# Weight decoding after attention: scaling and casts from GpSimd to ScalarE, a landing count for decode steps, two x pieces made early

## The chip, the cores and the metric

The kernel runs on one core of a Trainium2 chip. TensorE (PE) multiplies matrices; VectorE (DVE), ScalarE (ACT) and GpSimd (POOL) work elementwise; SyncE (SP) issues most DMAs. Each engine takes its instructions in program order, and an instruction that waits holds up all that stand behind it on its engine. The metric is the device time of one execution in microseconds (us).

## The reference

It computes three stages in float32 on 2304 tokens (4 batches of 576) of width 512.

```python
# attention with random features, 8 heads of 64, 128 features
q_p, k_p = phi(q * scale), phi(k * scale)   # phi: exp(proj - sq - max) / sqrt(m)
num = q_p @ (k_p^T v); den = q_p @ sum(k_p)
x = num / (den + 1e-6)
# block 1: 512 -> 2048 -> 512
h = x @ w_in
y = (max(h, 0) + alpha * min(h, 0)) @ w_out
# block 2: 512 -> 1536 -> 512
out = ((y @ w_a) * (y @ w_b)) @ w_out2
```

The weights reach the chip as 64-bit values, in which float64 bit patterns stand (`in_w`, two 32-bit words to each), and are turned to float32 on the chip.

## The kernel before

**Precision.** TensorE multiplies in a format of fewer bits, so each operand is split into a high piece (a cast) and a low piece (the rest), and each product takes three matmuls: high by high, high by low, low by high. `xh`/`xl`, `gh`/`gl` are such pairs; a weight's pair lies in a slot tile `w`.

**Stages.** First, attention steps run beside block 1's first 1280 tokens in chunks of 256 (object `A`, to about 256 us of the profile). Then block 1 goes on in chunks of 256 or 512 tokens (object `X`): tokens 1280 to 2303 with hidden blocks 0 to 7, then all tokens with blocks 8 to 15, to about 548 us. For each hidden block there are 12 matmuls into `h`, then ScalarE `u` and `h`, VectorE `h`, ScalarE `gh`, VectorE `gl`, and 12 matmuls into `y`, one or two blocks later. At the end of a chunk `y` is copied (`yo`) or added (`yp`). Last comes block 2, in three weight phases by three token groups of 768, nine groups in all: two times a `dual` (seven units of 12 matmuls, 384 wide, into the PSUM banks W, E and B, by a scheme of seven products instead of eight), then `back` (72 matmuls, 512 wide, into `o`). Sums `u`, `s`, `e` of those banks are copied by ScalarE and combined by VectorE.

**Decoder.** 68 weight pieces of 128x512 are decoded: SyncE loads `raw` (three buffers), GpSimd scales the high word into `z` (`start`), VectorE forms `a` and `c` by four instructions (`bits`), and then, for the first 32 pieces (`piece`), ScalarE casts the high piece and GpSimd or VectorE takes the difference and adds (`a<-a,w` and `w<-a,c`). For block 2 (`single`, and `quad` with sums of two pieces) a high piece is a GpSimd cast and the low piece a VectorE difference (`stage`); the pair goes straight into its slot where that is open, and else into a buffer `t` (three buffers), from there to DRAM (`store`, issued by `flush`), and later back into a slot (`fetch`).

**Order.** Every engine's order is that of the Python code. Decoding is a generator that is advanced between other work: after attention by `pace`, as long as VectorE's counted work is less than 1 us behind that of TensorE (`clock`, summed from fixed costs while the program is written). `pick` gives a difference to VectorE or GpSimd by the load counted for each. `upto` runs the generator until a piece that is needed is made.

Of the kernel before, what the change touches and what calls it, by code (L numbers as in the profile page):

```python
# [18 lines left out]
P = 128  # L19
# [15 lines left out]
CI = 256  # L35
# [24 lines left out]
FIRST = 32  # L60
SIDE = 0
# [3 lines left out]
def tile_kernel(ctx: ExitStack, tc: tile.TileContext, qT, kT, v1, omT, wbits, alpha, out):  # L65
# [106 lines left out]
    clock = {"pe": 0.0, "dve": 0.0}  # L172
# [26 lines left out]

    def behind():  # L200
        return clock["dve"] - clock["pe"]
# [3 lines left out]
    class Decoder:  # L205


        def __init__(self):
            self.free = {}
            self.raw = {}  # L210
            self.ready = 0
            self.made = set()
            self.next = 0
            self.credit = 0.0
            self.free_run = False
            self.gen = None
            self.z = {}
            self.ahead = True
            self.got = PB
            self.due = None  # L220
            self.direct = set()

        def load(self, i, after=False):
            if i < NP and i not in self.raw:
                raw = dec.tile([P, DM, 2], U32, tag="raw", name=f"raw{i}", bufs=3)
                if after:
                    after_dve(raw[:, :, 0].bitcast(F32))
                nc.sync.dma_start(out=raw.rearrange("p n t -> p (n t)"), in_=wbits[order[i]].bitcast(U32))
# [12 lines left out]

        def bits(self, i):
            self.start(i)
# [10 lines left out]
            if not fine and self.ahead and i + 1 < NP:  # L254
                self.start(i + 1)
# [18 lines left out]

        def stage(self, q, src, cut=None):

            if cut != 1 and self.open(q):
                self.direct.add(q)
            t = slots[place(q)][2] if q in self.direct else dec.tile([P, 2, 512], F32R, tag="t", name=f"t{q}_{cut}", bufs=3)
            if cut is not None:  # L280
                o = 256 * cut if q in self.direct else 0
                t = t[:, :, o:o + 256]
            self.flush()
            nc.gpsimd.tensor_copy(out=t[:, 0], in_=src)
            load["pool"] += 1.5
            yield
            yield
            vec(t[:, 1], src, t[:, 0].bitcast(F32), ALU.subtract)
            self.due = (q, cut, t)
            yield  # L290

        def flush(self):
            if self.due:
                q, cut, t = self.due
                if q not in self.direct:
                    dst = store[q] if cut is None else store[q][:, :, 256 * cut:256 * cut + 256]
                    nc.sync.dma_start(out=dst, in_=t.bitcast(F32))
# [8 lines left out]
        def single(self, i, q):  # L306
# [3 lines left out]
            self.start(i + 1)  # L310
            if self.kind(i + 1) == "quad":
                self.start(i + 2)
# [4 lines left out]
        def quad(self, i, q0, q1, q2, q3, m):  # L317
# [18 lines left out]
            self.start(i + 2)  # L336
            if self.kind(i + 2) == "quad":
                self.start(i + 3)
# [7 lines left out]
        def fetch(self):  # L346

            while self.got < PB + PH2 * QS:
# [3 lines left out]
                if q not in self.direct:  # L352
                    nc.sync.dma_start(out=slots[place(q)][2].bitcast(F32), in_=store[q])
# [69 lines left out]
        def upto(self, q):  # L423
            while q not in self.made:
                if not self.advance():
                    assert q in self.made, (q, self.next)
            if q >= PB:
                self.fetch()
                assert self.got > q, (q, self.got)
# [11 lines left out]
    class Mlp:  # L441
        def __init__(self, st, cap, ybufs, side=None):
# [4 lines left out]
            if not self.pair:  # L447
                self.px = pool(name=f"px{cap}", bufs=6)
            self.pg = pool(name=f"pg{cap}", bufs=3)
# [5 lines left out]
            self.xs, self.ys, self.gs, self.part = {}, {}, {}, {}  # L455
            self.half = {}
            self.q = []
            self.beside = None
            self.after = []
# [149 lines left out]
        def run(self, work, between, ready=lambda end, k: None):  # L609
# [8 lines left out]
            for ci, (ph, o, n, fs, lc) in enumerate(work):  # L618
# [8 lines left out]
                for i, f in enumerate(fs):  # L627
# [5 lines left out]
                    if i == 3 and ph == 1:  # L633
                        self.load_y(o, n)
            while self.q:
# [5 lines left out]
    st_a = ExitStack()  # L641
# [9 lines left out]
    pskv = rpool(st_a, name="pskv", bufs=1, space=PSUM)  # L651
# [230 lines left out]
    st_m = ExitStack()  # L882
    A = Mlp(st_m, CI, 2)
    st_z = ExitStack()
    psp[0] = rpool(st_a, name="ps", bufs=5, space=PSUM)
# [25 lines left out]
    with st_m:  # L911
# [35 lines left out]


# [16 lines left out]
        A.run(work0, beside, ready)  # L965
        while nxt_s[0] < steps:
            attn_more()
    st_a.close()
# [17 lines left out]
    def load_x(tp, k):  # L986
        stg = t_(xpools[0], f"st{k}", f"st{tp}_{k}", cols=4 * TN).rearrange("p (k n) -> p k n", k=2)
        nc.sync.dma_start(out=stg, in_=ypart[:, k::2, tp * 2 * TN:(tp + 1) * 2 * TN])
# [47 lines left out]
    st_w = ExitStack()  # L1036
    w2 = st_w.enter_context(tc.tile_pool(name="w2", bufs=1, side=RIGHT, reuse_waits="tile"))
    slots.update({i: pair_of(w2, i) for i in range(NS1, NS)})

    with ExitStack() as st:  # L1040
        X = Mlp(st, CB, 4, RIGHT)
# [15 lines left out]
    st_w.close()  # L1057
# [231 lines left out]
```

## Time and profile before

| what | value |
|---|---|
| median of 3 runs | 973.85 us (973.31 to 975.03) |
| the profiled execution | 974.33 us |
| its span | 972.6 us |
| PE busy in the span | 942.2 us, 97% |
| DVE, ACT, POOL busy | 71%, 48%, 29% |

The span reaches from the first to the last profiled instruction; 1.7 us of the execution's time lie around it. Matmuls overlap in the records, and one that runs slowly still counts as busy, so the busy share of PE alone does not tell how much time PE lost; the length of a stretch against its count of matmuls does.

### The profile page before, as it was taken

To read this page: it belongs to the slowest core of one execution; us is meant where nothing else is said; L and a number is where in the kernel's file an instruction comes from. 1 tells how busy PE (TensorE), PEld (TensorE's weight loads), DVE (VectorE), ACT (ScalarE), POOL (GpSimd) and SP (SyncE) were. 2 spreads that over 40 slices of the span, in tenths; PEclk is the share of its full clock that TensorE was granted. 3 is DMA by queue.
4 is the path that set the end of the run, shared out by engine and by line. 5 is a ranking of instruction groups with operands and counts; after the bars stand their busy time and mean duration, and the time that the engine had idled before them with its cause. 6 is when DMAs were issued, how large, how long until landed. Compare 5 with 4: busy or idle time off the path is not lost.

```text
span 972.6 us, 16848 instructions
## 1 busy us (share of the span) xinstructions
PE 942.2 (97%) x6486; PEld 844.3 (87%) x6486; DVE 691.9 (71%) x1348; ACT 462.4 (48%) x1130; POOL 282.8 (29%) x240
## 2 busy tenths in 40 slices
PE   7889999999999999999999999999999999999997
PEld 6778899989887878889888898999988899989895
DVE  5998855554498896678776978988675988274641
ACT  5877766654444534234334435443343443454532
POOL 3686710000088762122221201212234042110202
PEclk9999999999999999999999999999999999999999
DMA  7554322000133242315526665259837389623404
GB/s 297 167 161 148 132 75 78 23 24 24 44 95 122 87 149 65 112 38 169 203 103 251 223 227 205 88 206 393 317 108 218 111 216 351 191 38 93 56 11 65
DMA packets 49280, 138.15 MB, mean 142 GB/s; under 512 B 4528, under 2 KB 10928, under 8 KB 49200
## 3 DMA queue, kind: packets, MB, share of 16 engines
q1 hardware_dynamic: 43872, 127.51, 37.3%
q0 software_dynamic: 5184, 9.44, 6.5%
q8 instruction: 51, 0.84, 0.3%
q14 instruction: 29, 0.24, 0.1%
q10 hardware_dynamic: 144, 0.13, 0.0%
HBM read 89.87 MB, written 47.19 MB: 141 GB/s over the span
## 4 chain that ended last, share of the span: by engine, by line
PE 64%; DVE 12%; issue 8%; DMA 6%; ACT 4%; POOL 4%; SPq 0%; POOLq 0%; ACTq 0%; DVEq 0%
PE y L187 16%; PE h L187 15%; PE o L187 11%; PE W L187 9%; PE E L187 5%; DMA raw<-in_w 3%; PE B L187 2%; ACT ph L731 2%; DVE c L187 2%; DVE a L187 1%; DMA v<-in_v 1%; PE tp L187 1%; PE kv L187 1%; POOL z L237 1%; DVE z L187 1%
## 5 line engine op out<-in xcount | busy, mean ns | idle before, releaser
L187 PE MATMUL y<-gh,w 128*128 128x256 f32 (+1 forms) x768 | 203.1, 340 | 3.3 <-ACT gh L514 3.3
L187 PE MATMUL h<-xh,w 128*128 128x256 f32 (+1 forms) x768 | 204.5, 340 | 1.0 <-ACT xh L471 1.0
L237 POOL TENSOR_SCALAR z<-raw 128x512 f32<-128x512 f32 x68 | 113.6, 1671 | 197.4 <-DMA raw<-in_w 74.0
L187 PEld LDWEIGHTS y<-gh,w 128*128 128x128 f32 x768 | 135.3, 190 | 19.5 <-ACT gh L514 4.3
L187 PEld LDWEIGHTS h<-xh,w 128*128 128x128 f32 x768 | 135.0, 189 | 16.5 <-ACT xh L471 1.2
L187 PE MATMUL o<-w,gh 128*128 128x512 f32 x432 | 133.6, 390 | 0.7 <-ACT gh L162 0.7
L187 PE MATMUL y<-gl,w 128*128 128x512 f32 (+1 forms) x384 | 130.0, 339 | 0.5 <-DVE gl L187 0.5
L187 PE MATMUL h<-xl,w 128*128 128x512 f32 (+1 forms) x384 | 129.1, 336 | 0.5 <-DVE xl L475 0.5
L187 DVE SCALAR_TENSOR_TENSOR h<-u,nalpha,h 128x256 f32<-128x256 f32 (+1 forms) x96 | 59.6, 620 | 74.9 <-ACT h L502 73.3
L501 ACT ACTIVATE u<-h 128x256 f32<-128x256 f32 (+1 forms) x96 | 47.2, 491 | 121.7 <-PE h L187 121.5
L272 POOL TENSOR_TENSOR a<-a,w 128x512 f32<-128x512 f32 x32 | 46.7, 1460 | 183.4 <-ACT w L271 180.2
L187 PEld LDWEIGHTS o<-w,gh 128*128 128x128 f32 x432 | 80.7, 188 | 18.0 <-ACT gh L162 1.8
L514 ACT ACTIVATE gh<-h 128x256 fp32r<-128x256 f32 (+1 forms) x96 | 47.1, 491 | 82.9 <-DVE h L187 82.9
L187 PE MATMUL o<-w,gl 128*128 128x512 f32 x216 | 84.6, 391 | 0.3
L187 PEld LDWEIGHTS y<-gl,w 128*128 128x128 f32 x384 | 73.1, 190 | 8.8 <-DVE gl L187 1.4
L187 PEld LDWEIGHTS h<-xl,w 128*128 128x128 f32 x384 | 72.7, 189 | 8.5 <-DVE xl L475 1.0
L1191 POOL DMA_DIRECT2D out<-op x36 | 32.1, 910 | 161.9 <-ACT op L162 80.9
L187 DVE TENSOR_TENSOR gl<-h,gh 128x256 fp32r<-128x256 f32 (+1 forms) x96 | 53.0, 553 | 15.5 <-ACT gh L514 14.3
L162 ACT ACTIVATE u<-W 128x384 f32<-128x384 f32 x72 | 35.3, 492 | 60.3 <-PE W L187 59.4
L162 ACT ACTIVATE op<-o 128x512 f32<-128x512 f32 x54 | 32.1, 594 | 51.6 <-PE o L187 45.4
L187 DVE SCALAR_TENSOR_TENSOR a<-raw,z 128x512 uint32<-128x512 uint32 x68 | 54.6, 804 | 2.0
L187 DVE SCALAR_TENSOR_TENSOR c<-raw,c 128x512 f32<-128x512 uint32 x68 | 50.0, 735 | 2.3
(489 smaller groups left out, 1983.1 us busy)
## 6 DMA issues: line engine op xcount, KB each, us to landing
raw<-in_w SPq DMA_DIRECT2D x68, 512.0 KB, 4.2
w<-store SPq DMA_DIRECT2D x45, 512.0 KB, 7.5
store<-t_None SPq DMA_DIRECT2D x40, 512.0 KB, 3.4
st<-ypart SPq DMA_DIRECT2D x14, 768.0 KB, 7.5
out<-op POOLq DMA_DIRECT2D x36, 256.0 KB, 4.8
v<-in_v SPq DMA_DIRECT2D x8, 650.0 KB, 6.0
q<-in_qT SPq DMA_DIRECT2D x8, 576.0 KB, 3.7
out<-op SPq DMA_DIRECT2D x18, 256.0 KB, 2.2
```

Of the source, the lines that this page charges most:

```text
L162: nc.scalar.activation(out, in_, AF.Copy)
L187: return call(*a, **k)
L237: nc.gpsimd.tensor_scalar(out=z.bitcast(F32), in0=self.raw[i][:, :, 1].bitcast(F32), scalar1=2.0 ** -112, scalar2=None, op0=ALU.mult)
L272: eng.tensor_tensor(out=a, in0=a, in1=hi.bitcast(F32), op=ALU.subtract)
L501: nc.scalar.activation(u_, hp, AF.Relu, scale=-1.0)
L514: nc.scalar.activation(gh, hp, AF.Copy)
L731: nc.scalar.activation(ph[:, 2 * pr + j], pair[j][:, o + pr], AF.Exp, bias=nm[:, j, o + pr:o + pr + 1])
L1191: nc.gpsimd.dma_start(out=out[o:o + P, :], in_=op, accum_op=ALU.add)
```

## The change

From the end of attention on (`free_run`), ScalarE instead of GpSimd scales the exponent word into `z`, and `z` of the next piece is no longer made ahead. All casts in `stage` go to ScalarE. A second count, `clock["dma"]`, sums the bytes that are loaded or stored at 300 GB/s and adds 5 us (`LAND`); before a `z` is written out, and before a buffer `t` is taken again, the generator yields "wait" until TensorE's count has passed that time, unless `upto` forces it. This "wait" is a matter of the order in which instructions are written: the chip sees none of it. And `X`'s first tiles are allocated at the end of `A` (`over`), so that two of the four x pieces of `X`'s first chunk are made before `A`'s last matmuls are written.

```diff
+    def load_dma(out, in_):
+        n = size_of(out) * 4 * P if out.shape[0] == P else 0
+        clock["dma"] = max(clock["dma"], clock["pe"]) + n / 300e3
+        nc.sync.dma_start(out=out, in_=in_)
+        return clock["dma"] + LAND
...
@@ start
-            nc.gpsimd.tensor_scalar(out=z.bitcast(F32), in0=self.raw[i][:, :, 1].bitcast(F32), scalar1=2.0 ** -112,
-                                    scalar2=None, op0=ALU.mult)
-            load["pool"] += 0.8
+            high = self.raw[i][:, :, 1].bitcast(F32)
+            if self.free_run:
+                nc.scalar.activation(z.bitcast(F32), high, AF.Copy, scale=2.0 ** -112)
+            else:
+                nc.gpsimd.tensor_scalar(out=z.bitcast(F32), in0=high, scalar1=2.0 ** -112, scalar2=None, op0=ALU.mult)
+                load["pool"] += 0.8
@@ bits
+            self.load(i)
+            if self.free_run and i not in self.z:
+                yield from self.until(self.landed[i])
+                self.start(i)
+                yield
...
-            if not fine and self.ahead and i + 1 < NP:
+            if not fine and not self.free_run and self.ahead and i + 1 < NP:
                 self.start(i + 1)
...
+        def until(self, t):
+            while self.free_run and not self.force and clock["pe"] < t:
+                yield "wait"
@@ stage
+            if q not in self.direct and len(self.stored) > 2:
+                yield from self.until(self.stored[-3])
...
-            nc.gpsimd.tensor_copy(out=t[:, 0], in_=src)
-            load["pool"] += 1.5
+            act(t[:, 0], src)
@@ single and quad
-            self.start(i + 1)
-            if self.kind(i + 1) == "quad":
-                self.start(i + 2)
...
+        def over():
+            while nxt_s[0] < steps:
+                attn_more()
+            A.flush()
+            st_a.close()
+            mlp_x.append(Mlp(st_u, CB, 4, RIGHT))
+            for k in range(2):
+                mlp_x[0].split(0, CI * NCI, CB, k)
...
-        A.run(work0, beside, ready)
-        while nxt_s[0] < steps:
-            attn_more()
-    st_a.close()
+        A.run(work0, beside, ready, over)
+    st_p.close()
```

TensorE's order is the same in both programs, row by row. 50 of 68 `z` and all 60 casts move from GpSimd to ScalarE, eight `xl` pieces of block 1 from VectorE to GpSimd (by `pick`), and six pieces of block 2 go straight to their slots, so that SyncE has 228 rows instead of 240.

ScalarE's rows at the change from `A` to `X`; `gh0_1024_7` is the last one of `A`, `yo1024` its copies of `y`, `xh0_1280_0` to `_3` the high pieces of `X`'s first chunk. Before:

```order
L514 ACTIVATE gh0_1024_7_4077<-h0_1024_7_4060 128x256
L571 ACTIVATE yo1024_4117<-y0_1024_0_3911 128x256
L571 ACTIVATE yo1024_4117<-y0_1024_1_3912 128x256
L471 ACTIVATE xh0_1280_0_4164<-xT_75 128x512
L471 ACTIVATE xh0_1280_1_4168<-xT_75 128x512
L471 ACTIVATE xh0_1280_2_4172<-xT_75 128x512
```

And of the change:

```order
L539 ACTIVATE gh0_1024_7_4077<-h0_1024_7_4060 128x256
L496 ACTIVATE xh0_1280_0_4113<-xT_75 128x512
L496 ACTIVATE xh0_1280_1_4117<-xT_75 128x512
L596 ACTIVATE yo1024_4133<-y0_1024_0_3911 128x256
L596 ACTIVATE yo1024_4133<-y0_1024_1_3912 128x256
L496 ACTIVATE xh0_1280_2_4172<-xT_75 128x512
```

Two `xh` stand ahead of the copies now, two behind them as before.

GpSimd's rows at the end of `X`'s first chunk (tokens 1280 to 1791); the `xl` are low pieces for the next chunk. Before:

```order
L475 TENSOR_TENSOR xl0_1792_3_4492<-xT_75,xh0_1792_3_4491 128x512
L272 TENSOR_TENSOR a22_4448<-a22_4448,w22_4143 128x512
L273 TENSOR_TENSOR w22_4143<-a22_4448,c22_4449 128x512
L237 TENSOR_SCALAR z24_4509<-raw24_4446 128x512
L272 TENSOR_TENSOR a23_4506<-a23_4506,w23_4144 128x512
L273 TENSOR_TENSOR w23_4144<-a23_4506,c23_4507 128x512
L237 TENSOR_SCALAR z25_4539<-raw25_4504 128x512
```

And of the change:

```order
L500 TENSOR_TENSOR xl0_1792_3_4490<-xT_75,xh0_1792_3_4489 128x512
L290 TENSOR_TENSOR a22_4453<-a22_4453,w22_4154 128x512
L291 TENSOR_TENSOR w22_4154<-a22_4453,c22_4454 128x512
L290 TENSOR_TENSOR a23_4511<-a23_4511,w23_4155 128x512
L291 TENSOR_TENSOR w23_4155<-a23_4511,c23_4512 128x512
```

The two `z` have left GpSimd, and `z24` no longer stands behind the three `xl`.

Block 2, second weight phase. GpSimd's rows before, with `t75` to `t81` the high pieces of one `quad`, and `z62`, `z63` of the next:

```order
L1191 DMA out_0<-op1_2176_8735 128x512
L237 TENSOR_SCALAR z62_8798<-raw62_8721 128x512
L237 TENSOR_SCALAR z63_8800<-raw63_8757 128x512
L284 CAST t75_None_8808<-a60_8723 128x512
L284 CAST t76_None_8827<-c60_8724 128x512
L284 CAST t77_None_8861<-c61_8760 128x512
L284 CAST t81_0_8900<-a61_8759 128x256
```

The same casts in the change, on ScalarE, among the copies `op` of the output and the `xh` of the next token group:

```order
L163 ACTIVATE t75_None_9134<-a60_8860 128x512
L163 ACTIVATE t76_None_9157<-c60_8861 128x512
L163 ACTIVATE op1_1152_9160<-o1_1_3_9127 128x512
L163 ACTIVATE xh10A220_9167<-st0_0_8702 128x384
L163 ACTIVATE xh10A221_9169<-st0_1_8704 128x384
L163 ACTIVATE op1_1280_9178<-o1_1_4_9136 128x512
L163 ACTIVATE t77_None_9191<-c61_8915 128x512
L163 ACTIVATE op1_1408_9194<-o1_1_5_9143 128x512
L163 ACTIVATE t81_0_9212<-a61_8914 128x256
```

No `z` stands ahead of the casts any more: `z62` and `z63` follow later on ScalarE, among the bank copies of the next group.

## Rows read from the trace of the kernel before

**Rows 1.** The page, busy time by engine: us, share, instructions.

```profile
PE 942.2 (97%) x6486; PEld 844.3 (87%) x6486; DVE 691.9 (71%) x1348; ACT 462.4 (48%) x1130; POOL 282.8 (29%) x240
```

**Rows 2.** Windows: length, busy PE, PEld, DVE, ACT, POOL, granted clock, DMA share, GB/s.

```profile
256.30:263.85 7.55, 6.33 (x28) 4.86 (x27) 4.89 (x9) 4.15 (x8) 0.00 (x0) 1.00 0.45 141
309.69:314.65 4.96, 3.67 (x15) 2.52 (x14) 3.97 (x8) 3.16 (x6) 2.78 (x3) 1.00 0.72 220
355.06:362.37 7.31, 5.20 (x15) 3.64 (x14) 6.25 (x11) 3.75 (x7) 2.59 (x2) 0.77 0.55 185
548.50:578.45 29.95, 29.42 (x169) 29.08 (x168) 22.14 (x45) 13.70 (x31) 2.01 (x4) 1.00 0.67 240
578.45:595.88 17.43, 16.98 (x74) 13.36 (x73) 17.26 (x35) 9.82 (x21) 1.29 (x1) 1.00 0.26 88
595.88:625.02 29.14, 29.14 (x169) 29.14 (x168) 25.40 (x48) 12.69 (x27) 8.65 (x9) 1.00 0.51 174
625.02:641.38 16.36, 16.36 (x73) 13.52 (x73) 16.03 (x34) 8.88 (x19) 1.88 (x2) 1.00 0.35 137
716.04:733.40 17.36, 16.92 (x74) 13.36 (x73) 16.82 (x35) 10.25 (x22) 7.70 (x7) 1.00 0.39 81
733.40:783.47 50.07, 47.16 (x242) 42.38 (x241) 40.03 (x80) 21.23 (x46) 12.11 (x14) 1.00 0.56 159
256.00:548.00 292.00, 287.38 (x1347) 240.34 (x1347) 231.56 (x352) 117.50 (x225) 119.29 (x92) 0.99 0.39 132
548.00:966.00 418.00, 413.32 (x2163) 383.47 (x2162) 291.97 (x563) 178.82 (x378) 84.28 (x88) 1.00 0.55 171
```

**Rows 3.** The chain that ended last: start, length, what.

```profile
314.65 2.72 PE h L187 x12
```

**Rows 4.** Timeline, ScalarE at the start of `X`: start, length, instruction, count.

```profile
256.89 2.18 ACT L471 ACTIVATE xh<-xT 128x512 fp32r<-128x512 f32 x4
```

**Rows 5.** Timeline, GpSimd, VectorE, ScalarE near 300 us; in brackets idle before, releaser.

```profile
294.75 4.45 POOL L475 TENSOR_TENSOR xl<-xT,xh 128x512 fp32r<-128x512 f32 x3
...
303.84 1.50 DVE L187 TENSOR_SCALAR z<-z 128x512 uint32<-128x512 uint32 x1 [2.66 <-POOL z L237]
...
307.08 0.64 ACT L271 ACTIVATE w<-a 128x512 fp32r<-128x512 f32 x1 [8.29 <-DVE a L187]
```

**Rows 6.** Timeline, VectorE undisturbed at 262.93, and VectorE and ScalarE before 357 us.

```profile
262.93 0.42 DVE L187 TENSOR_SCALAR z<-z 128x512 uint32<-128x512 uint32 x1
...
351.58 1.51 DVE L187 TENSOR_SCALAR z<-z 128x512 uint32<-128x512 uint32 x1
...
355.91 0.74 DVE L187 SCALAR_TENSOR_TENSOR h<-u,nalpha,h 128x512 f32<-128x512 f32 x1
...
356.69 0.60 ACT L514 ACTIVATE gh<-h 128x512 fp32r<-128x512 f32 x1 [3.92 <-DVE h L187]
```

**Rows 7.** Timeline, GpSimd, VectorE and TensorE near 750 us.

```profile
748.61 1.51 POOL L237 TENSOR_SCALAR z<-raw 128x512 f32<-128x512 f32 x1 [4.27 <-DMA raw<-in_w]
...
750.71 1.06 DVE L187 TENSOR_TENSOR t_None<-a,t_None 128x512 fp32r<-128x512 f32 x1 [9.10 <-POOL t_None L284]
...
752.30 0.44 PE L187 MATMUL E<-xh11S,w 128*128 128x384 f32 x1 [2.07 <-DVE u L187]
```

**Rows 8.** Groups by line: busy us, mean ns | idle before; and DMA: KB, us to landing.

```profile
L237 POOL TENSOR_SCALAR z<-raw 128x512 f32<-128x512 f32 x68 | 113.6, 1671 | 197.4 <-DMA raw<-in_w 74.0
...
L271 ACT ACTIVATE w<-a 128x512 fp32r<-128x512 f32 x32 | 20.4, 636 | 16.7 <-DVE a L187 16.5
...
raw<-in_w SPq DMA_DIRECT2D x68, 512.0 KB, 4.2
```

**Rows 9.** Waits: who for whom, us in total, times, longest.

```profile
POOL z L237 <- DMA raw<-in_w: 74.0, 13, 16.2
...
POOL t L284 <- DMA store<-t_None: 50.7, 7, 22.7
...
DVE t_None L187 <- POOL t_None L284: 22.8, 9, 9.1
```

More of the change, by code (lines that the diff above doesn't have):

```diff
@@ L60 @@
 FIRST = 32
+LAND = 5.0
 SIDE = 0
@@ L170, in vec @@
         vector.tensor_tensor(out=out, in0=in0, in1=in1, op=op)
-    clock = {"pe": 0.0, "dve": 0.0}
+    clock = {"pe": 0.0, "dve": 0.0, "dma": 0.0}
     def size_of(ap):
@@ L221, in __init__ @@
             self.direct = set()
+            self.landed = {}
+            self.stored = []
+            self.force = False
         def load(self, i, after=False):
@@ L227, in load @@
                     after_dve(raw[:, :, 0].bitcast(F32))
-                nc.sync.dma_start(out=raw.rearrange("p n t -> p (n t)"), in_=wbits[order[i]].bitcast(U32))
+                self.landed[i] = load_dma(raw.rearrange("p n t -> p (n t)"), wbits[order[i]].bitcast(U32))
                 self.raw[i] = raw
@@ L296, in flush @@
                     dst = store[q] if cut is None else store[q][:, :, 256 * cut:256 * cut + 256]
-                    nc.sync.dma_start(out=dst, in_=t.bitcast(F32))
+                    self.stored.append(load_dma(dst, t.bitcast(F32)))
                 self.made.add(q if cut is None else (q, cut))
@@ L335, in quad @@
             vec(c1[:, g], a0[:, g], c0[:, g], sub)
-            self.start(i + 2)
-            if self.kind(i + 2) == "quad":
-                self.start(i + 3)
             yield
@@ L352, in fetch @@
                 if q not in self.direct:
-                    nc.sync.dma_start(out=slots[place(q)][2].bitcast(F32), in_=store[q])
+                    load_dma(slots[place(q)][2].bitcast(F32), store[q])
                 self.got += 1
@@ L448, in __init__, with rest @@
                 self.px = pool(name=f"px{cap}", bufs=6)
+            self.xs, self.ys, self.gs, self.part = {}, {}, {}, {}
+            self.half = {}
+            self.q = []
+            self.beside = None
+            self.after = []
+            self.open_ = lambda: self.rest(pool, ybufs)
+            if self.pair:
+                self.open_()
+        def rest(self, pool, ybufs):
+            cap = self.cap
             self.pg = pool(name=f"pg{cap}", bufs=3)
@@ L454, in __init__ @@
             self.banks = lambda h=None: self.open(pool, ybufs, h)
[L455 to L459, printed above, removed]
         def open(self, pool, ybufs, h):
@@ L607, in flush, with run @@
             self.after.clear()
-        def run(self, work, between, ready=lambda end, k: None):
+        def run(self, work, between, ready=lambda end, k: None, tail=lambda: None):
             def split(ph, o, n, k):
@@ L634, in run @@
                         self.load_y(o, n)
+            tail()
             while self.q:
                 self.pop()
-    st_a = ExitStack()
+    st_a, st_p = ExitStack(), ExitStack()
     def rpool(st, **kw):
@@ L880, in tile_kernel @@
     load_v(0)
-    st_m = ExitStack()
+    st_m, st_u = ExitStack(), ExitStack()
+    mlp_x = []
     A = Mlp(st_m, CI, 2)
     st_z = ExitStack()
-    psp[0] = rpool(st_a, name="ps", bufs=5, space=PSUM)
+    psp[0] = rpool(st_p, name="ps", bufs=5, space=PSUM)
     psx = st_z.enter_context(tc.tile_pool(name="psx", bufs=2, space=PSUM))
@@ L987, in load_x @@
         stg = t_(xpools[0], f"st{k}", f"st{tp}_{k}", cols=4 * TN).rearrange("p (k n) -> p k n", k=2)
-        nc.sync.dma_start(out=stg, in_=ypart[:, k::2, tp * 2 * TN:(tp + 1) * 2 * TN])
+        load_dma(stg, ypart[:, k::2, tp * 2 * TN:(tp + 1) * 2 * TN])
         stage_[k] = stg
@@ L1034, in begin @@
             next(first_x[0])
[L1036 to L1041, printed above, removed]
+    with st_u:
+        w2 = st_u.enter_context(tc.tile_pool(name="w2", bufs=1, side=RIGHT, reuse_waits="tile"))
+        slots.update({i: pair_of(w2, i) for i in range(NS1, NS)})
+        X = mlp_x[0]
+        X.open_()
         X.banks()
```

5 lines of the change are left out of this document (3 added, 2 removed).

## The prediction

> **What bounds the kernel now.** I read the busy shares first: PE is busy for 97% of the span, the next engine for 71% [rows 1]. TensorE's order is the same in both programs, row by row, so its work is fixed, and the change can only gain or lose what PE waits. Next I looked for those waits by the length of stretches with a known count of matmuls. The reader is to see the undisturbed pace first: 12 matmuls of 512 columns take 2.72 us in the chain, 0.227 each [rows 3]; in block 2 two `dual` take 29.14 us and a `back` 16.36 [rows 2]. Against these, the stretches after attention that are too long are, with what is lost in each [rows 2]:
>
> - (a) 256.30 to 263.85, the start of `X`: one matmul of 256 columns (about 0.12, an estimate by half of 0.227) and 24 of 512 (5.44) took 7.55, lost 1.99.
> - (b) 309.69 to 314.65: 13 matmuls (2.95) took 4.96, lost 2.01.
> - (c) 355.06 to 362.37: again 13 (2.95), took 7.31, lost 4.36.
> - (d) 548.50 to 578.45, the first `dual` pair: 29.95 against 29.14, lost 0.81.
> - (e) 578.45 to 595.88 and (f) 716.04 to 733.40, two `back`: 17.43 and 17.36 against 16.36, lost 1.07 and 1.00.
> - (g) 733.40 to 783.47, one whole group: 50.07 against 45.50, lost 4.57.
>
> Together that is 15.81 us, and no engine's share could gain more after 256 us. What stands before 256 us is untouched, since the new code asks for `free_run`; so is the tail behind the last matmul.
>
> Then I looked at what ends each wait, by timelines. In (a) ScalarE makes all four `xh` from 256.89 on, behind the copies `yo`, while PE stands [rows 4]. In (b) VectorE waits 2.66 us for GpSimd's `z`, which stands behind three `xl` of 4.45 us; ScalarE, waiting 8.29 us for `a` to cast `w`, holds the copies and `u` behind it [rows 5]. In (c) VectorE has a queue of decoding in front of `h`, with a `z` shift that takes 1.51 us instead of 0.42, so `gh` comes late [rows 6]; and the mean granted clock there is 0.77, so (1 - 0.77)/0.5 = 0.46 of 7.31 us, 3.4 us, ran at 1.2 instead of 2.4 GHz, which is some 1.7 of the 4.36 lost. In (g) GpSimd waits for a late `raw`, the cast `t` waits behind that `z`, VectorE waits 9.10 us for the cast with `u` behind it, and PE waits 2.07 us for `u` [rows 7].
>
> **The change part by part.**
>
> *Moved work.* 50 `z` of 1.67 us leave GpSimd [rows 8], and 60 casts. On ScalarE the nearest row is the cast `w<-a`, 0.64 us [rows 8]; at that price 110 instructions are 70 us at most. ScalarE has 117.5 of 292 us and 178.8 of 418 us busy in the two stages [rows 2], 296 of 710; with 70 more it is at 52%, so it does not become the bound by its share. This costs nothing as long as it lies in ScalarE's idle time; if it stood on the path it would cost 0.64 us each time.
>
> *(a)* Two `xh` and their `xl` are made before the copies. The third still starts behind the copies, near 256.9, and takes 2.18/4 = 0.55 us; its `xl` is a VectorE instruction of like length, so it is ready near 258.2, where PE, having done six matmuls of 0.227 from 256.4, wants it at about 258.0; the fourth likewise. Left over: 0 to 0.8, I take 0.3, gain 1.7.
>
> *(b)* `z24` stands on ScalarE behind `w23` and no longer behind the three `xl`, so the 2.66 us and the 8.29 us go. What then remains is the chunk's own chain (`yo`, `u`, `h`, `gh` against one group of 2.72). Left 0 to 2.0; I take 0.3, since the row of the cause is the `z` alone; gain 1.7.
>
> *(c)* One piece less is decoded in front of that `h` (`z32` and `a32` stand later), and one `xl` has moved to GpSimd. The 1.51 of `z32` alone brings `h` forward by that, `a32` and `xl` add as much again and more; the 2.7 us left beside the clock's 1.7 (4.36 - 1.7) are then covered, and with that wait I expect the low clock to go. Bounds: the wait goes and the low clock stays (gain 2.7), or all of it (4.36); below, if VectorE's queue stays long, 0. I take 4.0.
>
> By the Trainium skill (TensorE: Matmul & The Clock Gate, What's actually happening) the array runs at half clock unless recent activity releases it. The trace agrees at (c), 0.77, but the 2.07 us wait of (g) left 1.00 in its window [rows 2, 7]: a wait of this size does not always lower it.
>
> *(d), (e), (f)* Before the sums `yp` and before the bank sums VectorE has less decoding queued in the new order (a `quad`'s four sums stand behind `yp` instead of ahead; the `z48` group behind the first `back`'s sums; `t71` does not block), so most goes: 0 to 0.81, 1.07, 1.00; I take 0.5, 0.8, 0.7.
>
> *(g)* The casts `t75` to `t81` no longer stand behind two `z` that wait for `raw`; VectorE's 9.10 us go. Bounds 2.1 (the one wait) to 4.57; I take 4.2.
>
> *What it adds.* ScalarE now waits where GpSimd waited: for `raw` 74.0 us in 13 times, for a stored buffer 50.7 in 7 [rows 9]. Behind a waiting ScalarE stand `u`, `h`, `gh` and the bank copies, and PE behind those. The count with `LAND` is to keep such instructions from being written before the data is there: from a load to `z` it leaves 1.75 + 5 = 6.75 us of PE's counted time, against a median landing of 4.2 [rows 8]. Nor is a late piece free: the last one (`w5<-a67`) is written in the second `dual` of its first group, with some five of that `dual`'s seven units (2.08 us each, 29.14/14) still ahead of its `back`. Bounds of the new cost: nothing, or the 124.7 us of those waits. PE bore VectorE's 22.8 us of waits for casts in nine times [rows 9] at a loss of about 5.6 us, (f) and (g) together, a quarter; if a tenth of 124.7 is left over on ScalarE and a quarter of that reaches PE, 3 us; with that share no more than guessed I take 2.
>
> **The sum.** 1.7 + 1.7 + 4.0 + 0.5 + 0.8 + 0.7 + 4.2 = 13.6, less 2.0 is 11.6. Against the profiled execution's 974.33 us that gives 962.7; the median of the runs shown is 0.48 lower (973.85), so 962.2.
>
> **The rivals.**
>
> *VectorE stays late (R1).* GpSimd keeps `a<-a,w` and `w<-a,c` and gets eight more `xl`. VectorE's 1.51 instead of 0.42 [rows 6] was taken beside GpSimd's tensor work, and that remains. Then (c) gains only what the shorter queue gives, 1.5, and (d), (e), (f) nothing: 1.7 + 1.7 + 1.5 + 4.2 - 2.0 = 7.1, 966.8. Against it: (e), (f), (g) lie where GpSimd has no such work any more. The Trainium skill states the mechanism (SBUF — State Buffer, Who interferes with whom): a VectorE instruction with two SBUF inputs, or in a two-port mode, and a GpSimd instruction that reads SBUF lock each other out for a whole instruction. The trace agrees with it for that shift.
>
> *ScalarE is held (R2), the side that is slower.* The place is block 2 and the boundaries of chunks: casts wait for a store's landing or for VectorE's sum, `z` for `raw`, and bank copies stand behind them. GpSimd's longest such waits were 16.2 and 22.7 us [rows 9]. It decides when PE loses more than the 13.6 gained. At one wait in four left over at its mean (124.7/20 = 6.2 us, five times) and half of each reaching PE, 15.6 us are lost: 976.3. Against it: the count, and `z` that mostly stand much more than one load behind their `raw`.
>
> *Nothing comes of it (R3).* The waits are those of tight places (a chunk's end, the sums before `back`), and the decoding that is moved away comes back at the next: (a) and half of (g) are gained, the rest lost again, 4.0 - 2.0 = 2.0, so 971.9, or no change at all. For it: VectorE has 79% in `X` (231.56 of 292) and nothing of its own work is saved but contention [rows 2].
>
> **How the numbers follow.** Forecast 0.62 (959 to 966), R1 0.18, R3 0.12, R2 0.08. The likeliest gives 962.2. The lower end is all 15.81 regained at no new cost, 958.0, and a little for R3's and R2's low ends brings the upper end to 969.5, which takes in the forecast and R1. A measurement of this kernel tells 0.2% (1.9 us) from no change. Faster by more than that: forecast, R1 and half of R3, 0.86; slower: R2 and little of R3, 0.08; the rest, 0.06, within it.
>
> **What would show it.** In the new profile GpSimd has no scale or cast after 256 us, ScalarE about 360 us busy from there on; the window at `X`'s start is about 5.9 us instead of 7.55; the chunk starts near 305 and 350 keep PE without a wait above 0.5, at full clock; no `back` is over 16.7. R1 shows as VectorE releasing `gh` late at the second of these; R2 as ScalarE waiting for `raw` or `store` DMAs with PE behind; R3 as new PE waits of 1 to 3 us at other chunk ends. What would make me wrong most is a wait on ScalarE in front of bank copies, since each engine's queue is in order.

## The result, and the profile after

The changed kernel takes 961.83 us (median of four runs, 961.44 to 962.44) against 974.43 of the kernel before on the same chip (973.31 to 975.03): a ratio of 0.9873, 95% interval 0.9855 to 0.989. The profiled execution took 962.44 us with a span of 960.7.

The page, busy time by engine, as [rows 1]:

```profile
PE 937.1 (98%) x6486; PEld 843.7 (88%) x6486; DVE 671.4 (70%) x1340; ACT 517.9 (54%) x1240; POOL 168.1 (17%) x138
```

The windows between the same matmuls as the stretches (a) to (g) of [rows 2] and then the two stages; columns as there:

```profile
255.46:261.76 6.30, 6.08 (x28) 4.87 (x27) 2.60 (x5) 2.51 (x5) 0.00 (x0) 1.00 0.51 167
307.55:311.09 3.54, 3.48 (x15) 2.55 (x14) 2.13 (x4) 3.44 (x7) 1.97 (x2) 1.00 1.00 303
351.44:356.07 4.63, 3.77 (x15) 2.55 (x14) 2.56 (x5) 4.14 (x8) 2.00 (x2) 1.00 0.81 248
542.14:571.43 29.29, 29.29 (x170) 29.10 (x168) 23.07 (x48) 16.04 (x36) 0.00 (x0) 1.00 0.76 272
571.43:587.79 16.36, 16.36 (x73) 13.51 (x73) 16.19 (x35) 10.02 (x21) 0.00 (x0) 1.00 0.34 105
707.95:724.31 16.36, 16.36 (x73) 13.51 (x73) 16.16 (x34) 9.80 (x21) 3.88 (x5) 1.00 0.48 87
724.31:771.32 47.01, 45.80 (x241) 42.64 (x240) 37.21 (x76) 26.12 (x55) 5.16 (x7) 1.00 0.53 139
256.00:548.00 292.00, 291.09 (x1378) 245.01 (x1379) 222.70 (x351) 147.02 (x284) 60.23 (x44) 1.00 0.40 135
548.00:960.00 412.00, 404.31 (x2128) 377.83 (x2126) 278.98 (x553) 203.48 (x427) 31.57 (x36) 1.00 0.53 158
```

PE's order is the same row by row in every kernel here, so each trace can be cut at the same matmuls. The table does that: the seven stretches, then all the rest from the matmul that starts at 254.98 us in the kernel before to the last one, and that whole stretch; in us, by the starts of the matmuls. The experiments of the next section stand in it too. (Three stretches of the kernel before are 0.05 to 0.07 longer than in [rows 2], because the cut is at the start of the next matmul.)

| kernel | a | b | c | d | e | f | g | rest | whole |
|---|---|---|---|---|---|---|---|---|---|
| before | 7.60 | 5.03 | 7.37 | 29.95 | 17.43 | 17.36 | 50.07 | 575.48 | 710.29 |
| changed | 6.31 | 3.54 | 4.63 | 29.29 | 16.36 | 16.36 | 47.01 | 575.48 | 698.99 |
| after_again | 6.33 | 3.51 | 4.59 | 29.51 | 16.36 | 16.36 | 47.13 | 575.48 | 699.28 |
| late_x | 7.56 | 3.53 | 4.60 | 29.22 | 16.36 | 16.36 | 45.95 | 575.48 | 699.06 |
| z_gpsimd | 6.32 | 5.03 | 5.90 | 34.94 | 16.36 | 16.36 | 45.51 | 575.49 | 705.91 |
| cast_gpsimd | 6.31 | 3.53 | 4.61 | 29.42 | 16.36 | 16.36 | 45.51 | 575.48 | 697.60 |
| both_gpsimd | 6.31 | 5.05 | 7.29 | 29.97 | 17.35 | 16.36 | 47.11 | 575.49 | 704.91 |
| no_count | 6.32 | 3.51 | 4.59 | 29.34 | 16.36 | 16.36 | 51.78 | 575.49 | 703.75 |
| own_store | 6.32 | 3.52 | 4.61 | 30.35 | 16.36 | 16.36 | 45.51 | 582.00 | 705.03 |
| filler_gpsimd | 6.30 | 3.17 | 3.17 | 30.75 | 16.36 | 16.36 | 47.32 | 581.94 | 705.38 |
| filler_scalar | 6.30 | 3.93 | 4.95 | 31.17 | 16.36 | 16.36 | 47.08 | 581.23 | 707.38 |
| diff_vector | 6.30 | 3.17 | 3.17 | 29.35 | 16.36 | 16.36 | 45.51 | 591.28 | 711.51 |
| edge | 6.31 | 3.17 | 3.17 | 29.21 | 16.36 | 16.36 | 45.76 | 575.56 | 695.91 |
| best1 | 6.31 | 3.17 | 3.17 | 29.41 | 16.36 | 16.36 | 45.51 | 575.51 | 695.79 |

The change gains 1.29, 1.49, 2.74, 0.66, 1.07, 1.00 and 3.06 us, 11.3 in all, and nothing outside the seven stretches. The spans of the two profiled executions differ by 11.9 us: besides the 11.3, 0.85 lie in the first 40 us, where TensorE waits for the first loads (last section), and 0.26 is lost again behind the start of the last matmul.

What is left stands mainly in two places. One is (c). GpSimd, VectorE and ScalarE there, in that order; GpSimd's row is `a<-a,w` of the piece before:

```profile
345.00 1.66 POOL L290 TENSOR_TENSOR a<-a,w 128x512 f32<-128x512 f32 x1 [4.38 <-ACT w L289]
...
345.53 1.42 DVE L188 TENSOR_SCALAR z<-z 128x512 uint32<-128x512 uint32 x1
346.99 1.66 DVE L188 SCALAR_TENSOR_TENSOR a<-raw,z 128x512 uint32<-128x512 uint32 x1
...
351.80 0.60 ACT L539 ACTIVATE gh<-h 128x512 fp32r<-128x512 f32 x1 [4.36 <-DVE h L188]
```

A piece is still decoded in front of the copies and `h`, and beside GpSimd's instruction its first two steps take 1.42 and 1.66 us instead of 0.42 and 0.69, which is 1.97 us; `gh` is late by that much and the stretch is 1.46 above its floor of 3.17 (14 matmuls; edge and best1 below reach it). The other place is in (g). ScalarE's timeline there, and TensorE behind it:

```profile
731.16 0.62 ACT L163 ACTIVATE t_None<-c 128x512 fp32r<-128x512 f32 x1
737.34 0.42 ACT L163 ACTIVATE t<-a 128x256 fp32r<-128x256 f32 x1 [5.55 <-DMA store<-t_None]
737.66 0.85 ACT L163 ACTIVATE u<-W 128x384 f32<-128x384 f32 x2
...
738.18 0.44 PE L188 MATMUL W<-xh11A,w 128*128 128x384 f32 x1 [1.21 <-ACT u L163]
```

ScalarE waits for a buffer `t` to be stored, and the two bank copies `u` stand behind the cast; TensorE, which needs the bank, loses 47.01 - 45.51 = 1.5 us. In (a) about 0.5 is left over 5.8 (an estimate: one matmul of 0.12 and 25 of 0.227). It stands at the first `h`, where TensorE waits for VectorE's copy `yo` and not for the third `xh`:

```profile
255.95 0.50 PE L188 MATMUL h<-xh,w 128*128 128x512 f32 x1 [0.22 <-DVE yo L188]
```

What the moved instructions cost on ScalarE, by groups after 256 us:

```profile
L249 ACT ACTIVATE z<-raw 128x512 f32<-128x512 f32 x50 | 33.1, 662 | 0.0
...
L163 ACT ACTIVATE t<-a 128x256 fp32r<-128x256 f32 x10 | 4.1, 411 | 14.0 <-DMA store<-t_None 14.0
```

No `z` on ScalarE waits for a load any more (0.0; 74.0 us on GpSimd before, [rows 9]; in no_count below, without the count, it is 0.0 too), and of 50.7 us of waits for stores 14.0 are left.

### The profile page after: what moved, and what is told of

The parts are those of the page before. It is cut to its first block, busy times and chain, and to the rows that moved or that the text cites. A ratio compares the mean times of both kernels' runs of the same rounds, so it can differ in the third digit from the quotient of the medians.

```text
span 960.7 us, 16787 instructions
## 1 busy us (share of the span) xinstructions
PE 937.1 (98%) x6486; PEld 843.7 (88%) x6486; DVE 671.4 (70%) x1340; ACT 517.9 (54%) x1240; POOL 168.1 (17%) x138
## 4 chain that ended last, share of the span: by engine, by line
PE 77%; DVE 8%; issue 6%; ACT 5%; DMA 2%; POOL 1%; POOLq 0%; DVEq 0%; ACTq 0%
PE y L188 17%; PE h L188 17%; PE W L188 13%; PE o L188 13%; PE E L188 6%; PE B L188 3%; ACT ph L757 2%; DVE a L188 1%; DVE c L188 1%; PE tp L188 1%; DVE z L188 1%; PE kv L188 1%; DVE h L188 1%; PE nd L188 1%; DMA store<-t_None 1%
## 5 line engine op out<-in xcount | busy, mean ns | idle before, releaser
L188 PEld LDWEIGHTS h<-xh,w 128*128 128x128 f32 x768 | 135.0, 189 | 15.8 <-DVE yo L188 0.4
L188 DVE TENSOR_SCALAR z<-z 128x512 uint32<-128x512 uint32 x68 | 40.1, 589 | 24.6 <-ACT z L249 24.5
L188 DVE SCALAR_TENSOR_TENSOR c<-raw,c 128x512 f32<-128x512 uint32 x68 | 48.0, 707 | 2.3
```

The source lines that it names most:

```text
L188: return call(*a, **k)
```

## The experiments

Each was timed in five rounds beside the kernel before. Ratios are to the kernel before on the same chip; the kernel before came to 974.4 to 975.0 beside them, and since its single times scatter by 5 us and more, the stretches of the table decide.

**late_x**: the early x pieces undone.

```diff
-            for k in range(2):
-                mlp_x[0].split(0, CI * NCI, CB, k)
```

> The changed kernel, but all four x pieces of X's first chunk are made behind the copies, as before. Theory (the early pieces alone gave the 1.29 us that the start of X gained): about 1.3 us slower than the changed kernel's 961.8, 963.1, with ScalarE's four xh as one row before TensorE's first h of X, and nothing else moved. Rival (the start of X gained through other things, above all through z no longer standing on GpSimd, and the early pieces only change which piece is waited for): 961.8, within 0.3 us.

964.5 us, ratio 0.9892 (0.9867 to 0.9916). Stretch (a) is 7.56 instead of 6.31, and nothing else moves by more than 0.1 but (g), where ScalarE waits 4.51 instead of 5.55 us for the store and TensorE loses 1.06 less. The order there is the same; the store landed 7.83 us after its issue instead of 8.88. So the whole is equal to the changed kernel's, 699.06 against 698.99. The theory holds in its place: the early pieces are worth 1.25 us.

**z_gpsimd**: `z` back on GpSimd, one piece ahead as before.

```diff
-            if self.free_run:
+            if False:
                 nc.scalar.activation(z.bitcast(F32), high, AF.Copy, scale=2.0 ** -112)
...
-            if self.free_run and i not in self.z:
+            if False:
                 yield from self.until(self.landed[i])
...
-            if not fine and not self.free_run and self.ahead and i + 1 < NP:
+            if not fine and self.ahead and i + 1 < NP:
```

(and the calls of `start` in `single` and `quad` as before.)

> The changed kernel with z back on GpSimd and made one piece ahead, as before; casts on ScalarE, the early x pieces stay; the xl go back to VectorE by the load count. Theory (the gains at the chunk starts near 305 and 350 us and half of that of the long group near 740 come from z having left GpSimd): the waits at these two chunk starts come back, 1.5 and 2.7 us, and something of the 3.0 in the group, 966 to 969. Rival (the casts and the new order did it; z on GpSimd costs nothing as long as no cast stands behind it): 961.8 to 963.

972.01 us, ratio 0.9973 (0.9959 to 0.9986). (b) comes back in full, 5.03, and of (c) 1.27 of the 2.74. VectorE's rows in front of `h` in (c), now beside `a` and `w` on GpSimd twice over:

```profile
346.13 1.51 DVE L188 TENSOR_SCALAR z<-z 128x512 uint32<-128x512 uint32 x1
347.67 1.67 DVE L188 SCALAR_TENSOR_TENSOR a<-raw,z 128x512 uint32<-128x512 uint32 x1
...
350.77 1.52 DVE L188 TENSOR_SCALAR z<-z 128x512 uint32<-128x512 uint32 x1
352.32 1.66 DVE L188 SCALAR_TENSOR_TENSOR a<-raw,z 128x512 uint32<-128x512 uint32 x1
```

The expectation missed the larger part of the price: (d) takes 34.94, 5.65 more than in the changed kernel. (And (g), where it saw a loss, is at its floor of 45.51; TensorE comes 5.65 us later there.) ScalarE in that stretch:

```profile
564.00 0.52 ACT L163 ACTIVATE gh<-s 128x384 fp32r<-128x384 f32 x1
570.39 0.42 ACT L163 ACTIVATE t<-a 128x256 fp32r<-128x256 f32 x1 [5.87 <-DMA store<-t_None]
570.72 0.85 ACT L163 ACTIVATE e<-E 128x384 f32<-128x384 f32 x2
```

A cast on ScalarE waits for a store with bank copies behind it. In that trace the store issued at 560.1 lands at 570.3, behind two `st` loads and three fetches issued from 557.0 on.

**cast_gpsimd**: the casts back on GpSimd, `z` on ScalarE.

```diff
-            act(t[:, 0], src)
+            nc.gpsimd.tensor_copy(out=t[:, 0], in_=src)
+            load["pool"] += 1.5
```

> The changed kernel with the 60 casts of block 2's pieces back on GpSimd, z stays on ScalarE, so no z stands ahead of a cast. Theory (a cast was late because it stood behind a z that waited for its load): the casts alone cost little, the 1.4 us that TensorE loses in the changed kernel at 737 us, where ScalarE waits for a store with u behind it, even goes: 960 to 962.5. Rival (a cast on GpSimd takes 1.1 to 1.5 us, is slower still beside VectorE, and makes the sums before back late): 1.1, 1.0 and 1 to 2 us come back in block 2, 964 to 966.

961.93 us, ratio 0.9865 (0.9841 to 0.9889). (e) and (f) stay at 16.36, and (g) is at its floor, TensorE busy in all of it:

```profile
725.14:770.65 45.51, 45.51 (x241) 42.66 (x240) 39.60 (x76) 22.82 (x48) 9.19 (x13) 1.00 0.55 148
```

The theory holds. On GpSimd a cast still waits for its buffer, 36.9 us in five times, but nothing that TensorE needs soon stands behind it.

**both_gpsimd**: `z` and casts back on GpSimd (the two diffs above together); what is left of the change is the early pieces and that half of the count which holds back a buffer `t`; the half that holds back a `z` goes with the first diff.

> The changed kernel with z and the casts both back on GpSimd; the early x pieces and the count stay. Theory (each of z and casts alone may stand on GpSimd at the ends before back, since the two waits of 1.07 and 1.00 us there came only of casts standing behind z): with both there, these two waits come back, and the chunk starts lose 1.5 and 2.7 again; only the 1.3 at the start of X stays gained, about 1.3 below the kernel before, 972.5 to 973.5. Rival (the count and its order keep casts from standing behind z that wait): 966 to 970, without the two waits.

969.23 us, ratio 0.995 (0.9931 to 0.9968). The theory is right for (b), (c), (d) and (e), all within 0.1 of the kernel before, and wrong for (f) and (g). The windows of (c), (e), (f) and (g):

```profile
354.04:361.33 7.29, 5.17 (x15) 3.61 (x14) 6.23 (x11) 3.75 (x7) 2.61 (x2) 0.77 0.55 179
577.37:594.72 17.35, 16.94 (x73) 13.36 (x73) 17.18 (x35) 9.77 (x21) 1.72 (x1) 1.00 0.25 88
714.88:731.24 16.36, 16.36 (x73) 13.52 (x73) 15.20 (x28) 8.84 (x19) 7.00 (x8) 1.00 0.52 119
731.24:778.35 47.11, 45.80 (x242) 42.57 (x240) 38.51 (x77) 21.45 (x46) 11.10 (x14) 1.00 0.61 166
```

(f) is at its floor though GpSimd still waits 14.89 us for a `raw` in front of the cast. In the kernel before, VectorE's difference `t` waited 3.90 us for that cast at 713.32, with `u`, `s` and the `sumS` that `back` needs behind it; by that half of the count some decoding steps are written later (but for it and the early pieces, the order of every engine is that of the kernel before). VectorE's order there, buffer numbers left out, with the rows of the kernel before marked - and those of this one +:

```
-TENSOR_TENSOR t_None<-a,t_None 128x512
 TENSOR_TENSOR u_121<-E_121,u_121 128x384
...
 TENSOR_TENSOR gl<-w_121,gh 128x384
-TENSOR_TENSOR t_None<-c,t_None 128x512
 TENSOR_TENSOR xl11S<-sumS,xh11S 128x384
...
 TENSOR_TENSOR st_1<-st_1 128x384
+TENSOR_TENSOR t_None<-a,t_None 128x512
```

So the difference stands behind the sums now, and its wait costs nothing. The half of the count for buffers, with no work moved, is worth 1.00 + 2.96 us in (f) and (g).

**no_count**: the count away, the engines as in the changed kernel.

```diff
-            while self.free_run and not self.force and clock["pe"] < t:
+            while False:
```

> The changed kernel without the count of landings: z and casts are written as soon as the pace lets them. Only the order of the writing changes, from the middle of block 2 on, since the count holds a step back in only one place there. Theory (the count is nearly idle): 961 to 963. Rival (the count keeps ScalarE from being held, and without it ScalarE waits for a load or a stored buffer with bank copies behind it): 964 to 970, with a wait of ScalarE of over 5 us for a DMA.

969.01 us, ratio 0.994 (0.9921 to 0.996). The rival holds. Only (g) changes, 51.78 instead of 47.01. ScalarE, and TensorE behind it:

```profile
737.44 0.42 ACT L163 ACTIVATE t<-a 128x256 fp32r<-128x256 f32 x1 [7.21 <-DMA store<-t_None]
...
738.29 0.62 PE L188 MATMUL W<-xh11S,w 128*128 128x384 f32 x1 [4.42 <-ACT u L163]
```

Decoding is earlier there, and the cast that waits for a store stands in front of an earlier `u`. The first ScalarE row that stands elsewhere is a `z`, at 680.59 us and in front of two copies `s`; in the changed kernel it stands at 683.57, behind them. So with the work on ScalarE the one place where the count holds a step back, here by its half for `z`, is worth 4.8 us. The moved work without the count even makes (g) longer than in the kernel before, 51.78 against 50.07.

**own_store**: the count asks the store that frees the buffer.

```diff
-            if q not in self.direct and len(self.stored) > 2:
-                yield from self.until(self.stored[-3])
+            back = 2 if self.due and self.due[0] not in self.direct else 3
+            if q not in self.direct and len(self.stored) >= back:
+                yield from self.until(self.stored[-back])
```

> The changed kernel with the count for a buffer t taken from the store that frees it. Within a quad one finished buffer has not been stored yet when the count is asked, so the third last store is that of another buffer, one too early; here it is the second last in that case. Theory (the 1.4 us lost at 737 us, and the 14 us that ScalarE waits for stores, come of casts written one store too early): that wait goes, 959.5 to 961. Rival (the store is late since it stands behind two loads of 768 KB in the queue, which the count prices too low, and the pieces come later everywhere): within 0.5 of 961.8, or above it by a new wait for a piece.

970.64 us, ratio 0.9967 (0.9955 to 0.9979). The wait of (g) goes, 45.51. But waiting puts the whole decoder back: at 852 us TensorE waits for the cast of one of the last pieces, the rest is 6.5 longer, and (d) takes 1.1 more:

```profile
856.56 0.63 PE L188 MATMUL o<-w,gh 128*128 128x512 f32 x1 [4.37 <-ACT w L163]
```

The off-by-one in the count is real, and mending it alone costs 6 us.

**filler_gpsimd**: work for GpSimd that nobody needs.

```diff
+                for _ in range(4):
+                    nc.gpsimd.tensor_scalar(out=spare, in0=spare, scalar1=1.0, scalar2=None, op0=ALU.mult)
...
+            for _ in range(cols_of(src) // 128):
+                nc.gpsimd.tensor_copy(out=spare, in_=spare)
```

> The changed kernel, and GpSimd does work that nobody waits for in the places where z and the casts were: beside each z on ScalarE four scalings, beside each cast up to four copies, 128 columns each, of a scratch tile onto itself (what is computed stays the same). Theory C (GpSimd's work itself slows VectorE: z<-z 1.5 instead of 0.42 us): the waits at the chunk starts near 305 and 350 us come back in part, 1 to 3 us, and the sums before back get late, 0.5 to 2: 963 to 966. Theory Q (what counted was who stood behind whom on GpSimd): nothing waits for the filler but the differences a and w on GpSimd, 961.5 to 963.

970.54 us, ratio 0.9962 (0.9949 to 0.9975). Slower than either theory said, and in other places: not at the chunk starts, but in front of them, where `xl` on GpSimd stands behind the filler and TensorE waits for it in four places, 5.2 us in all; of the rest 1.5 are in (d). GpSimd, VectorE beside it, and TensorE's first wait:

```profile
296.28 3.45 POOL L252 TENSOR_SCALAR spare<-spare 128x128 f32<-128x128 f32 x4
299.69 4.37 POOL L506 TENSOR_TENSOR xl<-xT,xh 128x512 fp32r<-128x512 f32 x3
...
296.96 0.43 DVE L189 TENSOR_SCALAR c<-a 128x512 uint32<-128x512 uint32 x1
297.42 0.69 DVE L189 SCALAR_TENSOR_TENSOR c<-raw,c 128x512 f32<-128x512 uint32 x1
...
301.01 0.50 PE L189 MATMUL h<-xl,w 128*128 128x512 f32 x1 [1.28 <-POOL xl L506]
```

That is a queue: (b) and (c) are at their floor because TensorE is already late by then. And the filler is no substitute for the work that it stands for. VectorE's instructions beside it keep their length, as in the rows above; `z<-z`, where it runs beside nothing but filler, takes 0.41 to 0.53 us in all 17 places, not the 1.5 that theory C asked for. So it is not just any work of GpSimd that slows `z<-z`, which took 1.42 beside `a<-a,w` in (c), and this run does not tell the two theories apart.

**filler_scalar**: more work for ScalarE behind each `z` and cast.

```diff
+                for _ in range(4):
+                    nc.scalar.activation(spare, spare, AF.Copy)
...
+            for _ in range(cols_of(src) // 128):
+                nc.scalar.activation(spare, spare, AF.Copy)
```

> The changed kernel, and ScalarE does behind each z and each cast four (two) more activations of 128 columns of a scratch tile onto itself, so that what the change adds to ScalarE is there twice or more (what is computed stays the same). Theory (ScalarE has room; it is not the bound, and a longer instruction only costs where a bank copy stands right behind it): 962 to 964. Rival (ScalarE is near its bound at the chunk starts and in front of back; each instruction added there reaches TensorE): 966 or more.

971.89 us, ratio 0.9977 (0.9968 to 0.9986). The rival holds: the whole stretch is 8.4 us longer, most of it in a dozen places of 0.4 to 1.3 us. ScalarE is busy for 198.33 instead of 147.02 us from 256 to 548, at 68%, and for 258.67 of the 418 us up to 966; that is some 105 us more, and TensorE pays for one in twelve of them. ScalarE has room, but not between `h` and `gh` and not in front of bank copies.

**diff_vector**: the two difference instructions of a piece on VectorE after attention.

```diff
-            eng = (nc.gpsimd, vector)[way]
+            eng = vector if self.free_run else (nc.gpsimd, vector)[way]
```

> The changed kernel with both difference instructions of the pieces after attention on VectorE instead of GpSimd, so that GpSimd has no tensor work beside the decoding but xl. Theory C (what is left of the waits at the chunk starts, 0.6 and 1.6 us, comes of z<-z and a running beside GpSimd's a<-a,w, 1.42 and 1.66 us instead of 0.42 and 0.69): both waits go, though VectorE has some 30 us more to do: 959.5 to 961.5. Theory Q (VectorE's queue at the chunk's end is what is too long, and this makes it longer by 1.4 us): 963 to 966.

975.66 us, ratio 1.0014 (1.0002 to 1.0026). (b), (c) and (g) go to their floors, as theory C said. But the pace counts the added work on VectorE, lets the decoder fall back, and in block 2 the last pieces come late; TensorE's longest wait is this one:

```profile
850.26 1.52 PE L188 MATMUL o<-w,gh 128*128 128x512 f32 x2 [7.32 <-ACT w L163]
```

The rest is 15.8 us longer. Since the pace also left only one piece in front of `h` instead of two, this does not isolate contention either.

**edge**: in the last but one block of a chunk, no decoding after the first column group.

```diff
-                if not self.pair and e < 3 and not last:
+                if not self.pair and e < 3 and not last and not (ph == 0 and e and f == NF0 - 2):
```

> The changed kernel with one place less for decoding in the chunks of block 1's first half after attention: in the last but one block of a chunk no decoding after the first of its four column groups, so that the copies y and the next chunk's first h stand right behind the last gl on VectorE. Theory (what is left at the chunk starts, 0.6 and 1.6 us, comes of a piece decoded on VectorE there, beside GpSimd's a and w): both go, 959.5 to 961.5, and the pieces come no later, since the pace makes up for it. Rival (the pace gives the piece back a block later, at the same loss): within 0.5 of the changed kernel.

961.88 us, ratio 0.9865 (0.9846 to 0.9884). The theory holds: (b) and (c) are at 3.17, and no piece is late. Its profiled execution is 2.5 us shorter in span than the changed kernel's. Of the 3.1 us that the whole stretch gains (698.99 - 695.91), 1.25 are in (g), where this edit changes no engine's order: the wait of ScalarE for the store is there as before, 4.30 instead of 5.55 us, since the store landed 7.34 us after its issue instead of 8.88.

**after_again** and **best1**: the changed kernel once more, and the edits of cast_gpsimd and edge together.

> The changed kernel itself once more, as the measure for the three kernels beside it: 961.8, by the spread of the first 25 us between executions 961 to 964.

> The two edits that gained in the traces so far, together: casts on GpSimd with z on ScalarE (the wait of 1.4 us at 737 us went there), and no decoding behind the last but one block of a chunk, as in the kernel beside it. Theory (the two losses are apart, so the gains add): 3 to 3.7 us less than the changed kernel, 957.5 to 959.5. Rival (the casts on GpSimd come late once the order shifts, or a piece comes late in block 2's second or third weight phase, as in two kernels before): 961 to 968.

963.4 us, ratio 0.9887 (0.987 to 0.9904), and 959.36 us, ratio 0.9845 (0.9826 to 0.9864), on the same chip. Windows (b), (c) and (g) of best1:

```profile
306.73:309.90 3.17, 3.17 (x15) 2.63 (x14) 2.82 (x5) 2.14 (x5) 0.00 (x0) 1.00 0.53 189
350.25:353.42 3.17, 3.17 (x15) 2.63 (x14) 2.19 (x4) 2.13 (x5) 0.00 (x0) 1.00 0.54 189
721.80:767.31 45.51, 45.51 (x242) 42.66 (x240) 39.34 (x76) 22.81 (x48) 9.52 (x13) 1.00 0.57 148
```

TensorE is busy in all of each. Against after_again the whole stretch gains 699.28 - 695.79 = 3.5 us and the median 4.0, and (b), (c) and (g) give 0.34, 1.42 and 1.62 of it. That the gains add is not shown: edge alone stands at 695.91, 0.12 from best1, because its store landed early; why it did is open. What the casts on GpSimd buy is that (g) does not hang on that landing; in the four traces with the casts on ScalarE and the order of the changed kernel there (changed, after_again, late_x, edge), (g) lies between 45.76 and 47.13. By its median this is the fastest version found; of (d) to (g) only (d) is above the undisturbed pace of [rows 2], by 0.27.

## Why the prediction was right, point by point

The forecast was 962.2 us for the median, and it came out at 961.83. Such closeness is in part luck. The same kernel gave 963.4 in after_again; and in the stretches, which do not scatter so, the gain of 11.3 against the forecast 11.6 is made of misses that cancel: (a) to (c) brought 1.9 less than their terms, (d) to (f) 0.7 more, and (g) with the new waits 0.9 more. The prediction also counted a matmul too few in each of (a) to (c): TensorE starts 26 there in (a) and 14 in (b) and (c), so their floors are 5.8 and 3.17 instead of 5.56 and 2.95, and 15.3 us were there to be gained, not 15.81. Of the terms, measured in the table:

- **(a)**, 1.7: 1.29, and late_x shows that the early pieces alone gave it. Left over is 0.5, not the 0.3 taken, and in another place: TensorE waits for `yo` at the first `h`, not for the third piece. 6.30 to 6.33 is the length in every kernel with the early pieces.
- **(b)**, 1.7: 1.49, by `z` having left GpSimd (z_gpsimd).
- **(c)**, 4.0: 2.74. The step that failed is "the 2.7 us left beside the clock's 1.7 are then covered": only the low clock went, which cost 1.4 (last section) where 1.7 was estimated, and about half of the wait, 1.35 of 2.8. VectorE still decodes a piece in front of `h` beside GpSimd's `a<-a,w`, which was the mechanism of R1; R1's own price there, a gain of 1.5, was too low. By the Trainium skill (SBUF — State Buffer, Who interferes with whom) such a pair locks each other out for a whole instruction. The trace agrees with 1.42 and 1.66 us instead of 0.42 and 0.69, but the rows of filler_gpsimd show no such lock beside the filler. That the remainder is owed to it, and not to the length of the queue, is not isolated by a run: edge and diff_vector took both away.
- **(d), (e), (f)**, 0.5, 0.8, 0.7: 0.66, 1.07, 1.00. The mechanism given for (e) is borne out, with one thing not foreseen: it is enough that `z` leaves GpSimd, with the casts still there (16.36 in cast_gpsimd, 17.35 in both_gpsimd). The 16.36 of z_gpsimd shows nothing of that: the `z48` group stands ahead of the sums there as before, but TensorE is late from (d). The sums begin at 575.91 us and `back` at 581.16, in the kernel before at 576.24 and 578.45.
- **(g)**, 4.2, and the new waits, 2.0: 3.06 net, of which 1.5 is a new wait, so 4.56 gained. The size is right, the reason is not. The prediction took the gain of (g), and part of (f), for that of casts which no longer stand behind `z`. With both back on GpSimd they stand behind `z` again, and the two stretches still gain 1.00 and 2.96: the count does it, by the order it gives VectorE. In (f) the moved work does it too (16.36 in no_count); in (g) without the count it loses 1.71. The prediction had the count only as a guard against new waits.
- **New ScalarE waits**: the place is the one named, a wait of ScalarE in front of bank copies, for a store; 1.5 where 2.0 was guessed. The waits for `raw` that made up most of the 124.7 us went to nothing, since `z` is written no longer ahead; the count is not needed for that (0.0 in no_count too).
- **R2** did not happen, but it was closer than its 0.08: without the count's one held step it costs 4.8 us (no_count), and with `z` a piece ahead 5.65 in (d) (z_gpsimd). **R3** is excluded by the rest of the table, 575.48 before and after.
- Of what was to show it: no scale or cast is left on GpSimd, no `back` is over 16.7, and ScalarE has 147.02 + 203.48 = 350.5 us up to 960, of 360 forecast. Wrong were the window at `X`'s start (6.30, not 5.9) and the chunk start near 350, which loses 1.46, not less than 0.5.

So: of some 11.2 us (710.29 - 699.1, the mean of the two traces of the changed kernel) 1.25 to 1.3 are the early pieces, 4.0 the order that the count gives (f and g in both_gpsimd), and 5.8 (704.91 - 699.1) the work moved to ScalarE, with the low clock of (c) in it. The two kinds of moved work differ in sign. Moving `z`, with its half of the count, gains 7.3 (both_gpsimd to cast_gpsimd, 704.91 - 697.60); moving the casts costs 1.0 when `z` stays (z_gpsimd, 705.91) and 1.5 when it has moved (699.1 - 697.60). The shares hold for this order of undoing: with the work moved, the count is worth 4.8 (no_count).

## What to carry to other kernels

When a matmul-bound kernel loses a few us in a few places, cut both traces at the same matmuls: the stretches between them repeat to 0.05 us in two executions of one kernel, (d) and (g) to 0.2, where medians scatter by a us or two, and one run of each part undone then shows what the part is worth. In a queue that runs in order, put an instruction that may wait for a transfer where nothing urgent stands behind it: a slower, idle engine for the casts (GpSimd, 0.71 us in the mean for a 128x512 cast of `a` in cast_gpsimd) was better here than a faster, busy one (ScalarE, 0.63), by 1.0 to 1.5 us, or by 0.1 where the store landed early (edge). And a guard that makes the decoder wait is paid at the far end, when the last piece comes late.

## What the runs showed that was not expected

The same wait of TensorE lowered its clock in one kernel and not in another. In z_gpsimd and both_gpsimd the engines do the same in (c), and TensorE is idle for 2.12 us in each (5.90 - 3.78; 7.29 - 5.17), in a wait of 1.9 and one of 0.2, but the granted clock is 1.00 in the one and 0.77 in the other, and 1.4 us of the 2.74 gained in (c) hang on it:

```profile
354.25:360.15 5.90, 3.78 (x16) 2.55 (x14) 4.91 (x9) 3.16 (x6) 2.59 (x2) 1.00 0.48 179
```

By the Trainium skill (TensorE: Matmul & The Clock Gate, What's actually happening) recent activity decides on the throttle. These two traces agree that the length of the wait alone does not. What decided between them is open.

A store of 512 KB lands after 2.6 us when alone, as the one issued at 697.9 us in the changed kernel, and after 8.9 us when it is issued at 728.4, behind two `st` loads of 768 KB that were issued at 724.3 and 724.9 and land at 733.1 and 736.0. The count prices all at 300 GB/s; those two went at some 130 (1.57 MB in 11.7 us), with two output stores of 256 KB issued by GpSimd under way beside them (724.15 to 734.55 us).

Most of the scatter between executions lies in the first 40 us. The matmul that starts at 39.99 us in the kernel before starts between 38.31 and 41.55 in the other traces, while the 215 us behind it repeat within 214.97 to 215.03 in all fourteen. From the start of the last matmul to the end of the span it is 7.3 to 8.3 us.
